# Four weight loads at the start of an attention and gated feed-forward kernel, each issued as two transfers: rows 0 to 119 and rows 120 to 127

## The chip, the core and the metric

The kernel runs on one core of a Trainium2 chip. A core has a matrix engine (PE, with its weight loads shown apart as PEld), a vector engine (DVE), a scalar engine (ACT), a general engine (POOL, called gpsimd in the code) and a queue engine (SP), each with its own stream of instructions. They meet through semaphores. Transfers between the chip's main memory and the core's on-chip memory run on 16 DMA engines. The on-chip memory has 128 rows, called partitions; a tile's first dimension is the row.

The metric is the device time of one execution in microseconds. For the kernel before it is the median of three runs.

## The reference

For each of 8 batches b and 8 heads, with 576 positions, head size 64 and 32 memory slots:

```
a    = softmax(phi, over the 576 positions)            # 576 x 32
k_m  = a^T k ;  v_m = a^T v                            # 32 x 64 each
attn = softmax(q k_m^T / 8, over the 32 slots)         # 576 x 32
x    = attn v_m                                        # 576 x 64
```

The heads of a position are put side by side to a row of 512, which gives 4608 rows. On these a gated feed-forward block is computed, with an inner width of 1536:

```
out = (silu(x @ w_gate) * (x @ w_val)) @ w_out
```

All inputs and the output are float32.

## The kernel before

x is never formed. Since x = attn v_m for each head, the kernel multiplies v_m into the gate and value weights first: U = v_m W is small (32 slots of 8 heads against 1536 columns), and attn U is then the gate or the value. The function `u_round` (L460) makes U: its products (L472) write the tiles p_u from t_kT, the transposed memories, and W, the weights. `gv_half` (L509) makes gate and value, p_g and p_v, from t_A (attn) and t_U (L515), ACT applies silu (L532), DVE multiplies (L538). `products` (L689) multiplies the result by w_out by a scheme with fewer products than the plain one (L727), whose sums of operands POOL makes (L560, L603).

The order of the work is written out by hand, engine by engine in program order; nothing moves an instruction later on. The body first loads what batches 0 and 1 need (L885 to L916), with filler products on PE (`warm`, L867) where PE would otherwise stand idle, then runs batches 0 and 1 together (L921 to L971), and then batches 2 to 7 in a loop (L996).

The gate and value weights lie in main memory as 512 x 1536. They are loaded in three chunks of 512 columns, as bfloat16, by `load_w` (L128), from POOL's queue, since the type changes on the way. In on-chip memory a chunk has 128 rows and, in each row, four runs (the index i: row 128 i + p of the weights goes to partition p). Chunk 0 alone is split in two halves of 256 columns, so that the first products can start sooner:

```python
    for half in range(2):
        for which in range(2):
            load_w(which, 0, half)
    for c in range(1, NCH):
        for which in range(2):
            load_w(which, c)
```

The order on POOL's queue is therefore: k of batch 0, q of batch 0, k of 1, q of 1, v of 0, v of 1 (L99, L108, L103), then the first gate half, first value half, second gate half and second value half of chunk 0, then chunks 1 and 2 of gate and value, and then loads of w_out (L153), k, phi and v for batch 2. The framework gives POOL's transfers eight semaphores in turn. A transfer waits, on POOL, until the one eight places before it has landed; POOL goes through its stream in order, so all that is behind it waits too.

The first readers of W are the products of `u_half` (L836): L954 reads the first gate half, L956 reads the first value half and then both for batch 1, L963 reads the second halves for both batches, and `u_item(0, 1)` in L968 reads chunk 1, gate before value.

Of the kernel before, what the change touches and what calls it, by code (L numbers as in the profile page):

```python
# [14 lines left out]
def kernel(  # L15
# [19 lines left out]
    nc = tc.nc  # L35
# [13 lines left out]
    CH = 512  # L49
# [74 lines left out]
    W = {}  # L124
# [3 lines left out]
    def load_w(which, c, half=None):  # L128

        src = (moe_w_gate, moe_w_val)[which]  # L130
        split = half is not None
        if not half:
            W[which, c] = wpool.tile(
                [128, 2, NP, HC] if split else [128, NP, CH], BF16,
                tag=f"W{which}{c}", name=f"W{which}{c}",
            )
        f0, n = (half * HC, HC) if split else (0, CH)
        nc.gpsimd.dma_start(  # L138
            out=W[which, c][:, half] if split else W[which, c],
            in_=src[:, c * CH + f0:c * CH + f0 + n].rearrange("(i p) f -> p i f", p=128),  # L140
        )

    def w_part(which, c, i, g, halves):

# [760 lines left out]
# [6 lines that stand above are left out]
# [207 lines left out]
```

## Time and profile before

| What | Value |
|---|---|
| Median of three runs | 233.52 us (233.19 to 233.64) |
| The profiled execution, first to last instruction | 231.4 us |
| What lies around that span, by the median | 2.1 us |
| PE busy | 221.6 us, 96% of the span |
| DVE, ACT, POOL busy | 185.1, 171.7, 140.8 us |
| Granted clock of the matrix engine | 0.997 |
| A half chunk of gate or value weights | 256 KB on chip, 512 KB in main memory |
| Issue on POOL to landing, half chunks (median) | gate 19.3 us, value 18.7 us |
| One issue of a weight load on POOL | 0.74 to 0.77 us |

Times in the profile count from the first instruction. A line of the timeline has the start, the length, the engine, the source line, the operation, what it writes and reads, and, in brackets, how long the engine stood idle before it and what ended the idle time. The chain that ended last is followed back from the last instruction: at each step to what released it. The digits of the DMA row are the mean busy share of the 16 engines in tenths, in 40 slices of 5.8 us. POOL's busy time includes its issues of transfers.

### The profile page before, as it was taken

The numbers are of one execution on the slowest core, as the hardware profiler recorded it, in microseconds if no ns is written. First come the engines' busy times: TensorE is split into PE (matmuls) and PEld (weight loads), VectorE is DVE, ScalarE is ACT, GpSimd is POOL, SyncE is SP. The second block draws the span as 40 slices with busy tenths as digits, with TensorE's granted clock in tenths as the row PEclk, the third lists the DMA queues.
The fourth block names the chain that finished last, engine by engine and source line by source line (L and its number), as shares of the span: only waits on it lengthen the run. The fifth ranks groups of instructions, "written<-read, shape, count | busy, mean of one in ns | idle before, by whom it ended". The sixth has DMA issues, their size and how long they took to land.

```text
span 231.4 us, 7210 instructions
## 1 busy us (share of the span) xinstructions
PE 221.6 (96%) x2825; PEld 169.8 (73%) x2825; DVE 185.1 (80%) x423; ACT 171.7 (74%) x365; POOL 140.8 (61%) x190
## 2 busy tenths in 40 slices
PE   6987799999999999999999999999999999999993
PEld 2544476778887777878788787887788778878882
DVE  4245789999966799989997668998999899977732
ACT  2777898988447989968896658978898789677310
POOL 8422427998199049765977689464845394039291
PEclk9999999999999999999999999999999999999998
DMA  6999999999996992999299946994014502202125
GB/s 214 210 211 206 199 207 207 221 245 268 205 225 175 256 256 49 223 204 184 71 223 191 226 134 115 252 236 89 28 65 114 104 0 95 91 10 84 31 85 160
DMA packets 36674, 36.84 MB, mean 159 GB/s; under 512 B 14624, under 2 KB 31008, under 8 KB 36640
## 3 DMA queue, kind: packets, MB, share of 16 engines
q0 software_dynamic: 16272, 22.42, 52.5%
q1 hardware_dynamic: 19600, 13.18, 22.9%
q10 hardware_dynamic: 768, 0.79, 1.1%
q8 instruction: 22, 0.36, 0.6%
q14 instruction: 12, 0.10, 0.1%
HBM read 42.47 MB, written 9.44 MB: 224 GB/s over the span
## 4 chain that ended last, share of the span: by engine, by line
PE 86%; DMA 9%; POOL 2%; ACT 1%; issue 0%; DVE 0%; POOLq 0%
PE p_g L515 21%; PE p_os L727 21%; PE p_v L515 20%; PE p_oc L727 10%; DMA W<-in_moe_w_val_dram 9%; PE p_oa L727 5%; PE p_u L472 5%; PE p_kv L230 2%; PE p_g L396 1%; POOL t_kv L99 1%; POOL t_kv L103 1%; PE p_q L383 0%; POOL t_q L108 0%; ACT t_qT L337 0%; POOL W L138 0%
## 5 line engine op out<-in xcount | busy, mean ns | idle before, releaser
L538 DVE TENSOR_TENSOR t_h<-t_sg,p_v 128x288 bf16<-128x288 bf16 x192 | 81.8, 451 | 14.1 <-PE p_v L515 7.0
L515 PEld LDWEIGHTS <-t_U 128*128 128x128 bf16 x768 | 73.9, 98 | 21.2 <-issue 3.5
L532 ACT ACTIVATE t_sg<-p_g 128x288 bf16<-128x288 f32 x192 | 73.3, 424 | 17.1 <-PE p_g L515 11.4
L515 PE MATMUL p_g<-t_A,t_U 128*128 128x288 bf16 x384 | 77.0, 286 | 0.0
L515 PE MATMUL p_v<-t_A,t_U 128*128 128x288 bf16 x384 | 77.0, 286 | 0.0
L727 PEld LDWEIGHTS <-t_S 128*128 128x128 bf16 x384 | 37.5, 98 | 4.5 <-issue 0.2
L603 POOL TENSOR_TENSOR t_S<-t_h 128x512 bf16<-128x512 bf16 x17 | 19.7, 1157 | 32.7 <-DVE t_h L538 31.2
L727 PEld LDWEIGHTS <-t_h 128*128 128x128 bf16 x288 | 27.1, 98 | 8.6 <-issue 5.0
L492 ACT CAST t_U<-p_u 128x512 bf16<-128x512 f32 x51 | 27.0, 605 | 6.6 <-PE p_u L472 6.6
L727 PE MATMUL p_os<-t_T,t_S 128*128 128x256 bf16 x192 | 23.7, 273 | 0.0
L560 POOL TENSOR_TENSOR t_S<-t_S,t_h 128x512 bf16<-128x512 bf16 x17 | 19.6, 1156 | 1.3
L560 POOL TENSOR_TENSOR t_S<-t_h 128x512 bf16<-128x512 bf16 x16 | 18.4, 1152 | 0.0
L560 POOL TENSOR_TENSOR t_S<-t_h,t_S 128x512 bf16<-128x512 bf16 x16 | 18.4, 1152 | 0.0
L472 PE MATMUL p_u<-W,t_kT 64*32 64x512 bf16 (+1 forms) x416 | 15.3, 363 | 1.2 <-DMA W<-in_moe_w_gate_dram 0.6
L496 DVE CAST t_U<-p_u 128x512 bf16<-128x512 f32 x21 | 13.6, 683 | 1.9 <-PE p_u L472 1.9
L727 PE MATMUL p_os<-t_T,t_h 128*128 128x256 bf16 x96 | 14.8, 273 | 0.0
L875 PE MATMUL p_warm<-bones 128*128 128x512 bf16 x44 | 12.5, 421 | 1.7 <-DVE bones L897 1.7
L452 DVE TENSOR_TENSOR t_A<-t_E,t_lz 128x576 bf16<-128x576 bf16 x16 | 11.4, 740 | 0.7 <-ACT t_lz L428 0.7
L727 PE MATMUL p_oc<-t_T,t_S 128*128 128x256 bf16 x96 | 11.9, 273 | 0.0
L727 PE MATMUL p_oa<-WO,t_h 128*128 128x256 bf16 x96 | 11.8, 273 | 0.0
L727 PE MATMUL p_oc<-WO,t_S 128*128 128x256 bf16 x96 | 11.8, 272 | 0.1
L727 PE MATMUL p_os<-WO,t_h 128*128 128x256 bf16 x96 | 11.8, 273 | 0.0
(107 smaller groups left out, 308.3 us busy)
## 6 DMA issues: line engine op xcount, KB each, us to landing
out_dram<-t_o SPq DMA_DIRECT2D x11, 512.0 KB, 3.0
t_kv<-in_k_dram POOLq DMA_DIRECT2D x8, 576.0 KB, 10.5
t_q<-in_q_dram POOLq DMA_DIRECT2D x8, 576.0 KB, 8.4
t_kv<-in_v_dram POOLq DMA_DIRECT2D x8, 576.0 KB, 14.7
t_phi<-in_phi_dram POOLq DMA_DIRECT2D x6, 576.0 KB, 8.1
out_dram<-t_o SPq DMA_DIRECT2D x10, 256.0 KB, 4.5
WO<-in_moe_w_out_dram POOLq DMA_DIRECT2D x3, 512.0 KB, 19.2
W<-in_moe_w_gate_dram POOLq DMA_DIRECT2D x2, 512.0 KB, 16.5
```

Source lines behind the costliest of these rows:

```text
L230: nc.tensor.matmul(p[g][32 * i:32 * i + 32, 0:n], lhsT=phi_of(b, g, j, i), rhs=kvs[b][64 * g:64 * g + 64, w0:w1, i, j * D:(j + 1) * D], st ...
L452: nc.vector.tensor_tensor(out=a, in0=es.pop((b, g)), in1=lzs.pop((b, g)), op=ALU.mult)
L472: nc.tensor.matmul(p[g][32 * i:32 * i + 32, o:o + n], lhsT=kTs[b][64 * g:64 * g + 64, 2, 32 * i:32 * i + 32], rhs=w_part(w, c, i, g, halve ...
L492: nc.scalar.copy(out=t, in_=p)
L496: nc.vector.tensor_copy(out=t, in_=p)
L515: nc.tensor.matmul(p[:, 0:HALF], lhsT=Us[b, c, g][:, o // 2, which, 128 * (o % 2):128 * (o % 2 + 1)], rhs=atts[b, g][:, r], start=(g == 0) ...
L532: nc.scalar.activation(out=sg, in_=gate[:, 0:HALF], func=AF.Silu)
L538: nc.vector.tensor_tensor(out=dst, in0=sg, in1=val[:, 0:HALF], op=ALU.mult)
L560: eng.tensor_tensor(out=out, in0=x, in1=y, op=ALU.subtract)
L603: eng.tensor_tensor(out=t[:, 0], in0=A21, in1=A22, op=ALU.add)
L727: nc.tensor.matmul(mine[home][:, u], lhsT=lhs(c, m, u), rhs=rhs(c, m), start=fresh and u == 0, stop=(k == 5), skip_group_check=u == 1 or n ...
L875: nc.tensor.matmul(p[:, 0:128 * a], lhsT=bones, rhs=x.to_broadcast([128, a, 128]) if a > 1 else bones, start=True, stop=True,)
```

## The change

Where `load_w` loads a half chunk, it issues two transfers in place of one, the first for partitions 0 to 119 and the second for partitions 120 to 127. Source, destination, type and total bytes are the same. Whole chunks are loaded by one transfer as before. In all, four transfers become eight.

```diff
         f0, n = (half * HC, HC) if split else (0, CH)
-        nc.gpsimd.dma_start(
-            out=W[which, c][:, half] if split else W[which, c],
-            in_=src[:, c * CH + f0:c * CH + f0 + n].rearrange("(i p) f -> p i f", p=128),
-        )
+        dst = W[which, c][:, half] if split else W[which, c]
+        rows = src[:, c * CH + f0:c * CH + f0 + n].rearrange("(i p) f -> p i f", p=128)
+        for part in (slice(0, 120), slice(120, 128)) if split else (slice(0, 128),):
+            nc.gpsimd.dma_start(out=dst[part], in_=rows[part])
```

In program order POOL then has four more transfers between v of batch 1 and chunk 1. With eight semaphores in turn, the transfers behind wait for other ones than before: the 120 rows of the first value half wait for k of batch 0 (the whole first value half had waited for none), and chunk 1 of the gate weights waits for the 120 rows of the first gate half (it had waited for k of batch 1). The other whole chunks and the next loads likewise wait for a part of a half chunk; from the third load of w_out on, each transfer waits for the same earlier one as before. Products that read rows 64 to 127 wait for the second transfer also. The order and number of all other instructions is unchanged on every engine.

## The prediction

> **What bounds the kernel now.** I read the page's busy shares first, then the chain that ended last in order of time, then PE's timeline around the place where that chain leaves PE, and last the timeline of POOL, which issues these loads. The chain says where a microsecond is still worth a microsecond.
>
> ```profile
> PE 221.6 (96%) x2825; PEld 169.8 (73%) x2825; DVE 185.1 (80%) x423; ACT 171.7 (74%) x365; POOL 140.8 (61%) x190
> DMA  6999999999996992999299946994014502202125
> ```
>
> ```profile
> 6.04 0.72 POOL W L138
> 6.75 19.95 DMA W<-in_moe_w_val_dram
> 26.71 0.04 issue
> 26.75 0.52 PE p_u L472 x24
> 27.27 1.09 PE p_g L515 x8
> ```
>
> PE is the bound from 26.75 us on: the windows 26.75 to 54, 54 to 100 and 100 to 228 us have PE busy for 27.25 of 27.25, 45.90 of 46.00 and 127.60 of 128.00 us. Before that the chain is a single DMA, the first half chunk of the value weights, issued at 6.75 and waited for until 26.75. Whatever moves that landing moves the end by as much, as nothing behind it has room to take it up. The DMA row shows that the queues are full over the same time.
>
> ```profile
> 24.67 0.61 PE L875 MATMUL p_warm<-bones 128*128 128x512 bf16 x2
> 25.92 0.30 PE L472 MATMUL p_u<-W,t_kT 64*32 64x256 bf16 x8 [0.65 <-DMA W<-in_moe_w_gate_dram]
> 26.75 0.52 PE L472 MATMUL p_u<-W,t_kT 64*32 64x256 bf16 x24 [0.52 <-DMA W<-in_moe_w_val_dram]
> ...
> 29.75 0.63 PE L472 MATMUL p_u<-W,t_kT 64*32 64x256 bf16 x32
> ...
> 34.70 0.62 PE L472 MATMUL p_u<-W,t_kT 64*32 64x512 bf16 x16
> ```
>
> PE has nothing left at 25.28 (24.67 + 0.61), waits 0.65 us for the first gate half and 0.52 us for the first value half: 1.17 us is all that any earlier landing could give. The next two groups that read weights, at 29.75 and 34.70, start without a wait.
>
> ```profile
> 6.02 0.76 POOL L138 DMA_DIRECT2D W<-in_moe_w_gate_dram  x1
> 6.75 0.77 POOL L138 DMA_DIRECT2D W<-in_moe_w_val_dram  x1
> 9.19 0.75 POOL L138 DMA_DIRECT2D W<-in_moe_w_gate_dram  x1 [1.67 <-DMA t_kv<-in_k_dram]
> 12.00 0.74 POOL L138 DMA_DIRECT2D W<-in_moe_w_val_dram  x1 [2.06 <-DMA t_q<-in_q_dram]
> 14.82 0.74 POOL L138 DMA_DIRECT2D W<-in_moe_w_gate_dram  x1 [2.08 <-DMA t_kv<-in_k_dram]
> 18.40 0.74 POOL L138 DMA_DIRECT2D W<-in_moe_w_val_dram  x1 [2.83 <-DMA t_q<-in_q_dram]
> ```
>
> POOL keeps eight of its transfers in flight: the ninth, at 9.19, waits until the first has landed, and so on. Between issue and landing of the weights lie 15.5 to 20.0 us (the view of the tile W): they stand in a full queue.
>
> The trace also records sixteen completions for each transfer, one a DMA engine. Those of four weight transfers (us):
>
> ```
> first gate half   24.0 to 24.3 (fourteen), 25.1, 25.8
> first value half  25.3 to 25.6 (fourteen), 26.5, 26.7
> second value half 27.9 to 28.4 (fourteen), 29.2, 29.4
> second value chunk 33.1 to 33.4 (thirteen), 34.2, 34.5, 34.5
> ```
>
> PE waits for the last of sixteen. Fourteen engines are 1.1 us ahead of the sixteenth. The reason is in the records of the queue of instruction fetches: one 16 KB packet of 0.95 us at 14.63 and another of 0.94 us at 23.70. Up to the transfer that lands at 14.5 us no engine is behind; after the first packet one is by 0.8, after the second two are, and a third after the packet at 31.48. So the late engines are whichever served a fetch.
>
> **The change, part by part.** *Packets.* Each half chunk is 128 rows by four runs, 512 packets of 512 B (the four make the 2048 such packets of the queue), 32 an engine. Packets of an engine start 41 ns apart, and 32 of them are the 1.3 us by which the landings above follow each other. The same 512 packets are sent after the change. What moves is who sends them. No transfer of 120 or of 8 rows is in this trace. Its nearest row is the 128-row transfer, whose rows go evenly, eight to an engine; by it 120 rows fill fifteen engines as before and the sixteenth has none, and the 8 rows are one more row (four packets, 0.164 us) on each of eight engines. That is the value I take. The lower end is a gain: the engine without rows is a late one. The upper end is eight rows on one engine, or 120 rows on eight: 1.31 us a half chunk.
>
> *Completions.* A transfer ends with a 4 B packet on each engine, 21 ns in the queue. One more a half chunk: 0.02 us.
>
> Together a late engine among those eight has its landing later by 0.185 us a half chunk: 0.37 us at the first value half, 0.74 us at the second and at everything behind it.
>
> *PE.* The first value half ends at 26.73 + 0.37 = 27.10 and PE starts 0.37 later. The second value half is read from 29.87 and lands at 29.43: 0.44 us of room, and PE itself is 0.37 later, so 0.74 fits in 0.81. The second value chunk is read from about 34.99 (34.70 and the eight gate products before it, 0.28) and lands at 34.54: 0.45 of room, plus 0.37, holds 0.74 too. The four added semaphore waits on PE are met by then at no cost; if they were not, each is the landing already counted. The third chunk is read at 43.38 and lands at 39.6: covered by nearly 4 us.
>
> *POOL and its queue.* Four more issues, each between 0.55 us (the q load of 128 packets) and 0.77 us (512 packets). Their place in the eight in flight matters more. The first value half must now wait for the first k (issued at 9.19, before 6.75), the second gate half goes at 14.82 and 18.40, the second value half at 21.29 and 24.11, and the first whole gate chunk no longer at 14.82 but when the 120 rows of the first gate half have landed, 26.07. Behind it on POOL stand nine more loads, at 0.75 us each issued by 33 to 35, and no computing until 36.99. The queue must not run dry: the fourteen early engines end the second value half at 28.4. The first packet of a load into an empty queue came 1.3 us after its issue began (72.27 to 73.56), so the chunk issued at 26.07 starts at about 27.5, with 0.9 us in hand. Of an engine that did run dry, only a late one would count, and those have 1.1 us more work. I cost it at nothing; the cover is this 0.9 + 1.1 us. From the third load of w_out on (issued at 32.21), each load waits for the same earlier one as before. SP's first transpose waits for a q load that lands at 61.3 and for PE, and its output is read after 90 us: 0.74 later costs nothing.
>
> *Sum.* 0 for issue, 0.33 for packets, 0.04 for completions: 0.37 us on the span of 231.4, 231.8. The median of the timed runs stands 2.1 us above that span (233.52 against 231.4), which the change does not touch: 233.9 us, +0.16%.
>
> [...]
>
> **The rivals.** *It is hidden.* The late engines may be among the eight without an added row. Then the landing moves by the completions alone, 0.04 us, and the worst left is a third late engine at the second value chunk, 0.74 less the room of 0.45: 0.04 to 0.3 us, 233.6 to 233.8. For it: the trace does not name engines. Against: two late engines must both be spared.
>
> *It is faster.* The engine that loses its rows is a late one. One alone gives little: with the sixteenth completion of the first value half gone the fifteenth still stands at 26.5, a gain of 0.2 us at most. Only if both late engines are spared, for instance because the idle place moves from transfer to transfer, is the landing that of the other fourteen, 25.6 + 0.37 = 26.0: 0.75 us less, 232.8. It decides when the last completion comes before 26.25. For it: 1.1 us of lag really is there. Against: it is two engines, which change with the fetches.
>
> *The spread is uneven.* If 120 rows ran on eight engines (fifteen rows each), or the eight rows on one, the worst engine has 1.31 us more for each half chunk, 5.2 at the second value chunk; less 0.45 of room 4.8 us, or 3.7 where that engine was none of the late ones: 237.2 to 238.3. For it: a row count that is no power of two; against: 128 rows are spread evenly.
>
> *The queue runs dry.* If the small issues are much slower than 0.77 us, or the first half lands late, the first whole chunk is late by x. Up to about 2.4 us that is covered as worked out above, beyond it PE waits by the rest at 34.99: some 0.5 to 1.2 us, 234.0 to 234.7.
>
> **How the numbers follow.** About 0.2% (0.47 us) is what a measurement of this kernel can tell from no change; the three runs of before span 0.45 us. My forecast, a late engine with an added row, has 0.42: 233.5 to 234.4 on its own, so that 0.25 of it lies within 0.2% and 0.17 above. Hidden 0.18, all within. Faster 0.16, of which 0.14 beyond the bound. Uneven 0.16 and dry 0.08, all slower. So faster 0.14, same 0.45, slower 0.41. The range runs from the full relief (232.8, and 0.1 of spread) to 235.0, above the dry queue; the uneven case is left out.
>
> **What will show it.** Right: PE's first p_u group of values starts at 27.0 to 27.2, the group at 29.75 is later by the same amount and still has no wait, the POOL row for the first whole gate chunk stands near 26, and PE has as much work after it as before. Two late completions of sixteen, some 0.2 us later for each half chunk. Wrong: a start before 26.5 (relief), a wait on W before the groups that stood at 29.75 and 34.70 (uneven), a stretch between 27 and 30 us in which the DMA row falls (dry). What I know least is which engines get the eight rows; the fetches may also fall on other moments in other executions, which would move the lag of 1.1 us itself.

## The result, and the profile after

The changed kernel takes 234.06 us (median of 11 runs, 233.51 to 235.2) against 233.23 us for the kernel before on the same chip (11 runs, 233.06 to 233.64): 0.83 us longer, a ratio of 1.0035 with a 95% interval of 1.0025 to 1.0045. The sign and the mechanism of the forecast held, the size did not: 0.37 us were forecast. That the time still fell near the forecast of 233.9 is in part luck: that was counted from a median of three runs, 233.52, which stands 0.3 us above the 11.

The profiled execution took 233.92 us, with a span of 232.1 us, 0.7 us more than the span before. From its page, the busy shares, the DMA row and the packets:

```profile
PE 222.2 (96%) x2825; PEld 169.9 (73%) x2825; DVE 185.2 (80%) x423; ACT 171.5 (74%) x365; POOL 143.1 (62%) x194
DMA  6999999999997993899199965994023602202125
DMA packets 36994, 36.84 MB, mean 159 GB/s; under 512 B 14944, under 2 KB 31328, under 8 KB 36960
```

The work is the same but for POOL's four more issues. The page of the kernel before has 36674 packets: 320 more now, all of them under 512 B, and as many bytes. The chain that ended last, from its beginning (start, length, what):

```profile
1.25 7.78 DMA t_kv<-in_k_dram
9.03 0.28 issue
9.31 17.81 DMA W<-in_moe_w_val_dram
27.12 0.04 issue
27.16 0.78 PE p_u L472 x24
27.94 1.09 PE p_g L515 x8
```

As before it leaves the DMA at the first value half. That it now begins with k, for which the issue at 9.31 waited, looks like a new cause; an experiment below (112 and 16 rows) has the same issues and no loss clear of the noise. What counts is where the chain turns to PE. PE's timeline there:

```profile
25.10 0.60 PE L875 MATMUL p_warm<-bones 128*128 128x512 bf16 x2
26.05 0.50 PE L472 MATMUL p_u<-W,t_kT 64*32 64x256 bf16 x8 [0.35 <-DVE t_kT L339]
27.16 0.78 PE L472 MATMUL p_u<-W,t_kT 64*32 64x256 bf16 x24 [0.61 <-DMA W<-in_moe_w_val_dram]
...
30.43 0.63 PE L472 MATMUL p_u<-W,t_kT 64*32 64x256 bf16 x32
...
35.37 0.63 PE L472 MATMUL p_u<-W,t_kT 64*32 64x512 bf16 x16
```

The weight loads of the group of 24, before and after:

```profile
26.75 0.24 PEld L472 LDWEIGHTS <-t_kT 64*32 64x32 bf16 x23 [0.71 <-issue]
27.42 0.24 PEld L472 LDWEIGHTS <-t_kT 64*32 64x32 bf16 x23 [1.06 <-DMA W<-in_moe_w_val_dram]
```

The group of 24 starts 0.41 us later than before (26.75), close to the forecast of 27.10. But it also takes 0.78 us where it took 0.52. One product, on rows 0 to 63, starts at 27.16, when the 120 rows have landed; the second, on rows 64 to 127, starts at 27.42, when the 8 rows are there. The merged PE line hides this second wait in a longer group; the line of the weight loads shows it. The next two groups are 0.68 and 0.67 us later than before, without a wait. So the first value half is late by 0.67 us, and nothing after it is worse. POOL's timeline of the loads:

```profile
9.31 0.78 POOL L141 DMA_DIRECT2D W<-in_moe_w_val_dram  x1 [1.91 <-DMA t_kv<-in_k_dram]
12.12 0.55 POOL L141 DMA_DIRECT2D W<-in_moe_w_val_dram  x1 [2.03 <-DMA t_q<-in_q_dram]
...
26.20 0.79 POOL L141 DMA_DIRECT2D W<-in_moe_w_gate_dram  x1 [1.01 <-DMA W<-in_moe_w_gate_dram]
26.98 0.76 POOL L141 DMA_DIRECT2D W<-in_moe_w_val_dram  x1
```

The first whole gate chunk is issued at 26.20 (forecast 26.07). An issue of 8 rows took 0.55 us, one of 120 took 0.78. The completions of the sixteen engines, from the trace (us):

```
                             before                       after
first value half (120 rows)  25.3 to 25.6, 26.5, 26.7     24.8, 24.8, 25.3 to 25.8, 27.0, 27.1
  its 8 rows                                              25.0, 25.0, 25.6 to 26.0, 27.2, 27.4
second value half, 8 rows    27.9 to 28.4, 29.2, 29.4     27.6, 27.8, 27.9, 28.5 to 28.9, 29.9
gate chunk 1                 30.5 to 30.9, 31.7, 31.9     31.3 to 31.6, 32.2, 32.3, 32.6
```

(The second value half of before is one transfer of 128 rows.) Of the first gate half one engine is ahead (23.3, the next at 24.0), of the first value half two (24.8, the next at 25.3), of the 8 rows of the second value half three (27.6 to 27.9, the next at 28.5). The trace does not name engines; this is read as the engine without rows not always being the same. At the first value half two engines are late, as before, and later still. The fourteenth completion is 0.40 us later than before (26.02 for 25.62), and the last is 1.36 us behind the fourteenth where it was 1.09: 0.40 and 0.27 make the 0.67. At the second value half only one engine is left late. In the stretch from 27 to 29 us the queue thins out; the windows by engine (busy us, the granted clock, the DMA share and GB/s at the end), of the kernel before:

```profile
27.00:29.00 2.00, 2.00 (x39) 1.46 (x16) 1.78 (x4) 1.85 (x6) 1.37 (x2) 1.00 1.34 203
```

and of the changed one:

```profile
27.00:29.00 2.00, 1.84 (x34) 1.15 (x34) 1.90 (x4) 1.30 (x4) 2.00 (x3) 1.00 1.24 147
```

147 GB/s instead of 203: the first whole chunk came too late to keep the queue full. Its first packets start at 27.7, when an engine reaches them, but some of them take up to 0.98 us, where before each takes 0.10. This is not a matter of the engines without rows alone: with 112 and 16 rows, where no engine runs ahead, it is 146 GB/s. Everything behind in the queue then lands some 0.7 to 1.1 us later (v of batch 2 at 55.2 instead of 54.3).

### The profile page after: what moved, and what is told of

Read it like the earlier page. It is cut to its first block, busy times and chain, and to the rows that moved or that the text cites. A ratio compares the mean times of both kernels' runs of the same rounds, so it can differ in the third digit from the quotient of the medians.

```text
span 232.1 us, 7214 instructions
## 1 busy us (share of the span) xinstructions
PE 222.2 (96%) x2825; PEld 169.9 (73%) x2825; DVE 185.2 (80%) x423; ACT 171.5 (74%) x365; POOL 143.1 (62%) x194
## 4 chain that ended last, share of the span: by engine, by line
PE 86%; DMA 11%; ACT 1%; issue 0%; DVE 0%; POOLq 0%
PE p_g L515 21%; PE p_os L727 21%; PE p_v L515 20%; PE p_oc L727 10%; DMA W<-in_moe_w_val_dram 8%; PE p_u L472 5%; PE p_oa L727 5%; DMA t_kv<-in_k_dram 3%; PE p_kv L230 2%; PE p_g L396 1%; PE p_q L383 0%; ACT t_qT L337 0%; ACT t_p L752 0%; DVE t_q L339 0%; PE p_S L258 0%
## 5 line engine op out<-in xcount | busy, mean ns | idle before, releaser
L472 PE MATMUL p_u<-W,t_kT 64*32 64x512 bf16 (+1 forms) x416 | 15.8, 363 | 1.0 <-DMA W<-in_moe_w_val_dram 0.6
```

What stands on the lines that cost most here:

```text
L472: nc.tensor.matmul(p[g][32 * i:32 * i + 32, o:o + n], lhsT=kTs[b][64 * g:64 * g + 64, 2, 32 * i:32 * i + 32], rhs=w_part(w, c, i, g, halve ...
```

## The experiments

Two theories stood against each other at first. *Rows:* rows are dealt out whole, and what costs is that 120 and 8 rows do not fill sixteen engines evenly. *Transfers:* the four more transfers, their issues, or the changed window of eight in flight cost. Twelve kernels were run, four of them on each of three chips; the kernel before ran beside each four.

**The changed kernel again (e0_again).** No edit.

> The changed kernel once more, all four half chunks as 120 and 8 rows, for a second profile beside the others of this group. Theory rows (the cost is the extra packets that a late DMA engine sends ahead of the first value half, and PE's wait for the second of the two transfers): PE's first value products again later than in the kernel before by 0.3 to 0.7 us, the 8 rows landing some 0.2 us behind the 120; 233.8 to 234.3 us. Theory window (eight transfers in flight, so that the first whole chunk is issued 11 us later and the DMA queue runs thin): the same total, but with PE waiting for the second value chunk.

Measured: 234.19 us (12 runs, 233.53 to 235.73) against 233.59 for the kernel before (35 runs, 233.02 to 234.43): ratio 1.0026 (1.0007 to 1.0044). The loss, 0.60 us, is there on a second chip, with a wide spread.

**112 and 16 rows (e1_112_16).**

```diff
-        for part in (slice(0, 120), slice(120, 128)) if split else (slice(0, 128),):
+        for part in (slice(0, 112), slice(112, 128)) if split else (slice(0, 128),):
```

> Each half chunk again as two transfers, but of rows 0 to 111 and 112 to 127, both multiples of sixteen. The number of transfers, their issues on POOL and their places among the eight in flight are those of the changed kernel. Theory rows: every engine keeps its eight rows, only completions of 0.02 us a transfer are added, so 0.04 to 0.1 us above the kernel before, 233.3 to 233.4 us, and no burst of short packets on an idle engine. Theory window, and a fixed cost for each added transfer: as slow as the changed kernel, 0.7 to 0.9 us above before.

Measured: 233.69 us, ratio 1.0001 (0.9989 to 1.0013). The line of its page:

```profile
DMA packets 36739, 36.84 MB, mean 159 GB/s; under 512 B 14689, under 2 KB 31073, under 8 KB 36705
```

That is 65 packets more than before; the completions of four more transfers make 64. The 256 further short packets of the changed kernel are gone. Both row counts divide evenly over sixteen engines. As many transfers, in the same order of issues, cost 0.10 us by the medians, which is not clear of nothing (-0.26 to +0.30 us), where the changed kernel beside it lost 0.60 (0.16 to 1.03). The two intervals overlap; the run with 124 and 4 rows below bears the theory of rows out at a size far beyond the noise. As the cause of the bulk of the loss, the theory of transfers falls.

One part of it stays. The first whole gate chunk is issued late here too (26.05), and the queue thins out without any engine running ahead:

```profile
27.00:29.00 2.00, 1.98 (x36) 1.33 (x35) 1.63 (x3) 1.42 (x4) 2.00 (x3) 1.00 1.16 146
```

In the two runs that follow, which split only half of the loads and issue that chunk at 21.4 and 21.7, the same stretch moves 202 and 199 GB/s, as before the change. So the thin queue comes with the late issue, and not with the uneven rows.

**Only the first, only the second halves split (e2_first, e3_second).**

```diff
-        for part in (slice(0, 120), slice(120, 128)) if split else (slice(0, 128),):
+        for part in (slice(0, 120), slice(120, 128)) if half == 0 else (slice(0, 128),):
```

The other one has `half == 1`.

> Only the first halves (the first gate half and the first value half) as 120 and 8 rows, the second halves whole. Theory rows: nearly the whole cost, 0.5 to 0.8 us, because these are the transfers ahead of the wait that sets the end. Theory window: none, since the first whole chunk now waits for v of batch 0 and is issued near 21 us. A fixed cost per transfer: half, 0.4 us.

> Only the second halves as 120 and 8 rows. Theory rows: the first value half lands as before, the second up to 0.4 us later into 0.44 us of room, so 0 to 0.1 us. Theory window: none, the first whole chunk is issued near 21 us. A fixed cost per transfer: 0.4 us if the room behind the first value half did not cover it.

Measured: first halves 233.81 us, ratio 1.0011 (0.9998 to 1.0023); second halves 233.65 us, 1.0003 (0.999 to 1.0016). The medians stand 0.22 and 0.06 us above before, 0.28 together, and the whole change 0.60 beside them. The order is the expected one (what PE waits for costs, what is covered does not), but neither differs surely from no change; the first halves were expected to cost 0.5 to 0.8 us and came out lower. The sum is less than the whole, though by the spread of these runs that could be chance. One thing that needs both is the late issue of the first whole chunk.

Where that can cost shows at 59 us, where PE transposes q of batch 2 (p_q, L383). In the kernel before, q lands at 58.63 and PE comes at 59.12, without a wait:

```profile
59.12 0.84 PE L383 MATMUL p_q<-ident,t_q 128*128 128x128 bf16 x12
```

In the profile of the changed kernel run again:

```profile
59.58 0.84 PE L383 MATMUL p_q<-ident,t_q 128*128 128x128 bf16 x12 [0.23 <-DMA t_q<-in_q_dram]
```

Here q lands at 59.53. The queue carries its delay of 0.9 us from the start for 30 us; PE in this execution was late by 0.17 only, and the room of 0.49 us is used up. The profile of 112 and 16 rows, with the same late chunk and no uneven rows, has such a wait too; q lands at 59.93 there:

```profile
59.98 0.84 PE L383 MATMUL p_q<-ident,t_q 128*128 128x128 bf16 x12 [0.35 <-DMA t_q<-in_q_dram]
```

**Fixing the place of the idle engine (f0_start0, f1_start4, f2_start8, f3_start12).** The theory, an assumption: the engine that gets no rows is the next in a turn that goes on from one execution to the next, so that the spread of the changed kernel comes from where the turn stands. A small transfer of 4, 8 or 12 rows, which nothing reads, is put ahead of the loads and another behind the last, so that by this theory all executions start alike:

```diff
+    def turn(n):
+        t = consts.tile([16, 16], FP32, tag=f"turn{n}", name=f"t_turn{n}")
+        nc.gpsimd.dma_start(out=t[0:n], in_=phi[0, 0, 0:n, 0:16])
```

The four have, ahead and behind: none and 4, 4 and none, 8 and 12, 12 and 8 rows.

> The changed kernel, and behind its last load one more transfer of 4 rows of 64 B that nothing reads. Theory turning: in the completions of the changed kernel one engine runs ahead after the first half chunk, two after the second, three after the fourth, so that the engines without rows change from transfer to transfer, 15 on for 120 rows and 8 on for 8 rows, 92 on in an execution, and the next execution begins elsewhere. With the 4 rows it is 96, a multiple of 16, and each execution begins in the same place as its first. Then the spread (2.2 us in twelve runs of the changed kernel on this chip) falls to that of the kernel before (1.4 us in 35) and the median lies near the first, profiled executions, 233.5 to 233.9 us. If the places do not turn between executions, spread and median stay as in the changed kernel, 234.0 to 234.3 with runs above 235. [...]

> The changed kernel with a transfer of 4 rows of 64 B, read by nothing, ahead of all loads of POOL: 96 places in an execution, so that every execution begins four places on. The eight in flight are as in the changed kernel, as this transfer lands long before its place is used again. Theory turning: a spread like that of the kernel before and a median of its own, between 233.4 and 235.5, and in the profile other engines are ahead and other ones late. Theory of no turning: 234.0 to 234.3 as in the changed kernel, with runs above 235.

> The changed kernel with 8 rows of 64 B ahead of all loads and 12 rows behind the last: 112 places in an execution, so that every execution begins eight places on. Theory turning: a spread like that of the kernel before and a median of its own, between 233.4 and 235.5. Where it is slow, the profile shows where: PE waits for the first value half by more than in the kernel before, or for the second value half, or for the second value chunk. Theory of no turning: 234.0 to 234.3 as in the changed kernel.

> The changed kernel with 12 rows of 64 B ahead of all loads and 8 rows behind the last: 112 places, every execution begins twelve places on. Theory turning: a median of its own between 233.4 and 235.5 with a small spread, and the mean of the four starting places is that of the changed kernel, 234.2. Theory of no turning: as the changed kernel.

Measured, against 233.5 us (35 runs, standard deviation 0.30): 234.3 (deviation 0.28), 234.65 (0.48), 233.98 (0.36), 234.22 (0.80); ratios 1.0033, 1.0049, 1.0025 and 1.0043, each within about 0.002. All four lose. Only one has the small spread that the theory asks for, and the last falls into two groups, seven runs from 233.76 to 234.33 and then four in a row from 235.49 to 235.68. The theory is not shown. Three of the four long runs list a granted clock of 0.989 to 0.992 where the first seven list 0.997 to 1.000, but the fourth lists 0.998; what sets the two groups stays open. The profiles are of use in another way: the last one has the largest wait for q of all,

```profile
60.16 0.84 PE L383 MATMUL p_q<-ident,t_q 128*128 128x128 bf16 x12 [0.74 <-DMA t_q<-in_q_dram]
```

where PE had been only 0.23 us late until then.

**Taking the second place away (g1_after_qfirst, and on the kernel before, g2_before_qfirst).** q of batch 2 is loaded ahead of phi of batch 3:

```diff
-        (0, 0): lambda: (load_phi(3, nc.gpsimd), load_q(2)),
+        (0, 0): lambda: (load_q(2), load_phi(3, nc.gpsimd)),
```

> The changed kernel with one line swapped: q of batch 2 is loaded ahead of phi of batch 3 instead of behind it, so that it should land about 2 us earlier than the 59.7 us of the changed kernel. Theory of two places (the late landing of the first value half, and again q of batch 2, which PE's transposes at p_q read about 59 us in): the second place is gone, no wait stands before the p_q transposes, VectorE's drift against the kernel before is as large at the end as it is at 28 us, and the median is 0.2 to 0.5 us above the kernel before, with few runs above 234.4. Rival, the first place alone carries the loss: the median stays 0.6 to 0.8 us above the kernel before, with the same tail up to 235.

> The kernel before with the same swapped line, nothing split: the control for the run beside it. Two places: q of batch 2 had 0.5 us of room here (landed 58.6, read 59.12), so the median stays within 0.2 us of the kernel before; a loss of its few runs near 234.4 would say that the same place makes those. Rival, the swap itself is worth something (the queue or PE's order changes by it): the median moves by more than 0.3 us, and the difference of the run beside it has to be read against this one.

Measured, against 233.31 us (23 runs, 232.97 to 234.43): changed kernel with the swap 233.83 (12 runs, 233.49 to 234.89), ratio 1.002 (1.0007 to 1.0034); kernel before with the swap 233.43, 1.0001 (0.9987 to 1.0014). The swap by itself does nothing, and the changed kernel still loses 0.52 us to before, 0.40 to its control. That is just above what was expected of two places (0.2 to 0.5) and just below what was expected of one alone (0.6 to 0.8). Against the 0.60 and 0.83 us of the changed kernel without the swap, the second place would be worth between 0.1 and 0.4 us of the median, but the intervals overlap, and these runs cannot tell it from nothing. The expected end of the tail did not come: the profiled execution is itself the longest, 234.89 us, and its lines say where that lies:

```profile
27.64 0.73 PE L472 MATMUL p_u<-W,t_kT 64*32 64x256 bf16 x24 [1.33 <-DMA W<-in_moe_w_val_dram]
...
60.22 0.84 PE L383 MATMUL p_q<-ident,t_q 128*128 128x128 bf16 x12
```

No wait at p_q (q landed at 57.66), and all of the loss at the first value half: its last rows landed at 27.81. Two engines were behind the others by 1.6 and 1.8 us there, where they were 0.8 and 1.1 behind in the kernel before; the first of them was behind fourteen of the others by 1.6 us already when v of batch 1 landed (0.8 before), after an instruction fetch at 14.83. The kernel before has such a fetch at 14.63; why the lag behind one is 1.6 us and behind the other 0.8 the trace does not show, nor that the fetch makes it.

Beside each other, twelve profiles show how strictly the first place works. The second column is the last of the sixteen completions of the first value half (of its second transfer, where there are two), the third how much later VectorE's first multiply of gate and value starts than in the kernel before, the fourth the same past 77 us, behind the second place:

| Kernel | Landed, us | Later at 28 us | Later past 77 us |
|---|---|---|---|
| before | 26.71 | 0 | 0 |
| before, q first | 26.57 | -0.14 | -0.14 |
| second halves only | 26.86 | 0.16 | 0.15 |
| first halves only | 26.86 | 0.16 | 0.16 |
| 112 and 16 rows | 27.14 | 0.44 | 0.86 |
| changed | 27.38 | 0.67 | 0.67 |
| changed, again | 26.87 | 0.16 | 0.46 |
| changed, none and 4 rows | 27.34 | 0.63 | 0.72 |
| changed, 4 and none | 27.24 | 0.53 | 0.57 |
| changed, 8 and 12 | 27.38 | 0.67 | 0.79 |
| changed, 12 and 8 | 26.93 | 0.23 | 1.03 |
| changed, q first | 27.81 | 1.10 | 1.10 |

The third column is the second less 26.71, within 0.02 us, in every row: PE's start follows the last landing one to one. The three kernels with an undivided first value half land at 26.71 on average, the seven changed ones at 27.28, 0.57 us later; past the second place those seven are 0.76 us late on average, against medians that stood 0.48 to 1.15 us above before. One profile says little: the seven, whose first halves are loaded alike, land anywhere from 26.87 to 27.81. The row of 112 and 16 is the exception among the even ones: 0.44 us late at the first place with no uneven rows. It is of an execution of 234.07 us, the second longest of its twelve, so the profiles alone do not tell it from the seven; the medians do that.

**124 and 4 rows (g3_124_4).**

```diff
-        for part in (slice(0, 120), slice(120, 128)) if split else (slice(0, 128),):
+        for part in (slice(0, 124), slice(124, 128)) if split else (slice(0, 128),):
```

> Rows 0 to 123 and 124 to 127 in place of 0 to 119 and 120 to 127, all four half chunks. Theory that whole rows are dealt out to a number of engines that divides the row count: 124 rows go as 31 rows on each of four engines, 124 packets of 41 ns (5.1 us) where there were 32 (1.3 us); the first value half lands some 6 to 8 us later, and with the four half chunks the median is 3 to 7 us above the kernel before; twelve engines without rows show as short packets, far more than the 320 of the changed kernel. Rival, rows are spread as evenly as the count allows (124 on sixteen engines, seven or eight each): it costs no more than the changed kernel, 0.4 to 0.9 us, with packets added by completions alone.

Measured: 241.4 us (4 runs, 240.31 to 242.21), ratio 1.0334 (1.0301 to 1.0367): 8.1 us longer. From its page:

```profile
DMA packets 42882, 36.86 MB, mean 153 GB/s; under 512 B 20832, under 2 KB 37216, under 8 KB 42848
```

6208 more packets than before. The trace does not name engines, but a count explains the number: if the 124 rows lie on four engines, 31 each, an engine sends 124 packets; if each of the other twelve sends as many short ones, and likewise 4 for the 4 rows, with 16 completions that is 1488 + 48 + 16 = 1552 a half chunk, and four times that is 6208. The same count for 120 rows (one engine idle, 32) and 8 rows (eight idle, 4 each) gives 32 + 32 + 16 = 80, and four times that is the 320 seen. The completions agree: of the first gate half twelve engines are done by 25.2, four at 28.2 to 28.5. PE's timeline:

```profile
28.63 1.63 PE L472 MATMUL p_u<-W,t_kT 64*32 64x256 bf16 x32 [2.90 <-DMA W<-in_moe_w_gate_dram]
30.19 2.10 PE L515 MATMUL p_g<-t_A,t_U 128*128 128x288 bf16 x8
...
36.15 1.22 PE L472 MATMUL p_u<-W,t_kT 64*32 64x256 bf16 x32 [1.38 <-DMA W<-in_moe_w_gate_dram]
...
43.24 0.62 PE L472 MATMUL p_u<-W,t_kT 64*32 64x512 bf16 x16
```

and its windows (the last three figures: granted clock, DMA share, GB/s):

```profile
25.80:27.30 1.50, 0.00 (x0) 0.00 (x0) 0.38 (x2) 0.76 (x1) 0.00 (x0) 1.00 1.35 108
27.40:34.20 6.80, 5.57 (x49) 3.13 (x50) 3.11 (x6) 3.49 (x8) 3.03 (x4) 0.50 1.17 125
34.30:37.60 3.30, 1.92 (x39) 0.90 (x38) 1.30 (x3) 0.77 (x2) 1.21 (x2) 1.00 1.43 166
37.70:41.00 3.30, 3.30 (x16) 2.12 (x14) 1.81 (x5) 2.40 (x6) 2.41 (x4) 0.50 1.23 205
41.10:43.00 1.90, 1.90 (x17) 1.52 (x16) 1.46 (x5) 1.60 (x4) 0.74 (x1) 1.00 1.23 204
```

The expectation had the count of engines right and the path wrong. The first value half landed at 29.4, 2.7 us later, not 6 to 8, and only 0.9 us behind the first gate half (28.5), where 124 packets of 41 ns behind those of the gate on the same engines would be 5.1. That is read as gate and value on different groups of four engines, side by side. PE's two waits, 4.28 us, are 3.1 more than the 1.17 of before. Most of the rest is clock. The granted clock fell to 0.50 at 27.4, inside the wait of 2.90 us, and stayed there to 34.2; it was 1.00 to 37.6, 0.50 again to 41.0, and 1.00 from then on. The eight gate products behind the first weight group took 2.10 us where they took 1.15. The same products between the first weight group and the one at 43.24 took 13.2 us without the wait between them, where they had taken 8.3. Of these 5.0 us about 4.5 are half of the 9.0 us in which PE was busy at half the clock, an estimate from the stretches above. The 5.0 us, the 3.1 us and 0.45 that PE was late already at 25.12 make the 8.5 us by which everything past 43 us is later in this execution.

**A version that might beat both (g4_v1_later).** The kernel before with the swap of q, and v of batch 1 loaded behind the first halves, its work on PE moved behind them:

```diff
     load_v(0)
-    load_v(1)
-    for half in range(2):
-        for which in range(2):
-            load_w(which, 0, half)
+    for which in range(2):
+        load_w(which, 0, 0)
+    load_v(1)
+    for which in range(2):
+        load_w(which, 0, 1)
...
-    v_direct(1, "vvvv")
-    warm(8)
...
-    run([u_half(0, (0,), 0, 0, "va")])
+    run([u_half(0, (0,), 0, 0, "vv")])
...
-    run([u_half(0, (1,), 0, 0, "va"), u_half(1, (0, 1), 0, 0, "av")])
-    for s in range(4):
+    run([u_half(0, (1,), 0, 0, "vv")])
+    for s in range(3):
         gv_gate(0, s)
+    v_direct(1, "vvvv")
+    gv_gate(0, 3)
...
+    run([u_half(1, (0, 1), 0, 0, "av")])
```

> The kernel before with the swapped line and the loads in another order: v of batch 0, the first gate and value halves, then v of batch 1, then the second halves; PE does the first gate and value halves of batch 0 and its gates, then the work on v of batch 1 that it had done ahead of them. If what bounds the start is the landing of the first value half, that lands by about the 0.7 us earlier that the v load took in the queue ahead of it (64 packets an engine), PE's work of the first value half starts at 25.9 to 26.2 instead of 26.75, and the time is 0.4 to 0.9 us below the kernel before. If the start is bound by PE, VectorE or the second halves as well, a new wait stands before the work on v of batch 1 or before the second halves, and the time is within 0.3 us or longer.

Measured: 234.73 us (5 runs), ratio 1.0051 (1.0033 to 1.0068), 1.4 us longer than before. PE's timeline:

```profile
23.93 0.41 PE L472 MATMUL p_u<-W,t_kT 64*32 64x256 bf16 x16
24.83 1.18 PE L515 MATMUL p_g<-t_A,t_U 128*128 128x288 bf16 x6 [0.49 <-DVE t_U L498]
26.65 0.76 PE L325 MATMUL p_mT<-t_mphi,t_kv 128*64 128x64 bf16 x36 [0.65 <-DMA t_kv<-in_v_dram]
...
29.68 0.62 PE L515 MATMUL p_g<-t_A,t_U 128*128 128x288 bf16 x2 [0.79 <-ACT t_U L494]
```

The first value half landed at 23.6, 3.1 us earlier (0.7 had been expected), and PE's work on it began 2.8 us earlier; three new waits (the copies of U on DVE and ACT, and v of batch 1, 1.93 us in all) and the moved work itself took more than that back: the group of both second halves starts at 30.96 where it started at 29.75. The rival that was named came true. Nothing run here beats the kernel before.

## Why the prediction was right and wrong

- *The chain leaves the DMA at the first value half, and its landing moves the end one to one:* right, and the table shows it twelve times.
- *Packets, 0.33 us, and completions, 0.04 us, at the first value half; PE 0.37 later:* the mechanism right, the term mis-sized. The packet counts (the 320) fit the spread assumed, 120 rows on fifteen engines and 8 rows one each on eight. The last 8 rows land 0.16 to 0.26 us behind the last of the 120, where four packets of 41 ns and a completion make 0.185. But the whole was 0.67 us in the profile of the changed kernel and 0.57 on average. The step that failed is that the lag of the late engines was taken as the 1.1 us of one profile, the same before and after. For the engines that are not late the term fits: the fourteenth completion is 0.40 us later in the changed kernel's profile, and 0.33 on average over the seven against the three with an undivided half. The lag of the last behind the fourteenth is what came on top: 0.27 us in that profile, 0.24 on average (1.10 for 0.87). It differs from execution to execution (one engine was 0.8 us behind after its first fetch in the profile of before, 1.6 in that of 234.89 us). With landings from 26.87 to 27.81, seven profiles cannot tell 0.57 from 0.37 with much confidence, nor whether the longer lag belongs to the change.
- *PE's start at 27.10:* met (27.16), but by luck: 27.10 was to be the landing of both parts, and 27.16 follows the landing of the 120 rows alone. PE does one product and waits again, until 27.42.
- *0.74 us is covered at the second value half and at the second chunk:* right; no wait at 30.43 and 35.37. The delays were 0.50 us at the half (29.91 for 29.41) and 0.99 at the second value chunk (35.46 for 34.47).
- *POOL costed at nothing, the first whole chunk near 26, the queue with 0.9 us in hand:* the issue came at 26.20, as forecast, but the 0.9 us did not keep the queue full. The sign named for a queue that runs dry, less traffic between 27 and 30 us, came: 147 GB/s for 203, and 146 with 112 and 16 rows. With those rows even the engine that is first has 3.14 us between the second value half and the first whole chunk, where it had 2.58. PE did not wait at the second value chunk for it; it can pay at q of batch 2, and the median of 112 and 16 rows puts it at 0.10 us, not clear of nothing.
- *"0.74 later costs nothing" for the loads further back:* this step was incomplete. It followed q of batch 3 to its first reader, and not q of batch 2, which has 0.49 us of room at 59.12. By the forecast's own numbers, 0.74 late against 0.49 of room and PE 0.37 late, there is no wait; but where PE is late by less than the queue (0.17 against 0.9, 0.23 against 1.5), the difference comes due there: 0.23 and 0.74 us. On average over the seven profiles the loss grows from 0.57 to 0.76 us past this place.
- *The base:* 2.1 us around the span came from setting the median of three runs against the span of one. The profiled executions since stood 1.8 us above their own spans.
- *The rivals:* hidden and faster did not come, though one, two and then three engines ahead can be read as the idle place moving from transfer to transfer, as the second assumed. Of the dry queue the thin stretch came and the wait at the second value chunk did not. Uneven spread: not at 120 and 8, but at 124 and 4 it came, 8.1 us; the argument for it, a count that is no power of two, was the wrong test, since 112 is none either and cost 0.10 us, not clear of nothing.

## What to carry to other kernels

Before a load is cut in two, measure what the row counts do: here 112 and 16 rows cost nothing that could be measured (ratio 1.0001), 120 and 8 some 0.6 to 0.8 us, 124 and 4 8.1 us, with the same bytes and the same number of transfers; only the first pair divides evenly over sixteen engines. When a full queue gets later, follow the delay to every later load that has less room than the delay, tens of microseconds on (here q of batch 2, 0.9 late with 0.49 of room at 59 us), and not only to the next few. And where the last of sixteen landings sets the end, one profile is one draw: the changed kernel landed 0.5 us apart in two executions (27.38 and 26.87), and its variants with the same first loads up to 0.9.

## What the runs showed of the hardware that was not expected

- The split into 120 and 8 rows brought short packets beside its completions: between 20 and 30 us the POOL loads of the changed kernel show 401 packets of 4 B, those of the kernel before 81, and 252 of the 401 took 9 ns, a length that none of the 81 has (of the completions before most took 22 ns). That the engines without rows send them, each as many as the others send packets with data, is read from the counts above, 320 and 6208, which come out exactly so; the trace does not name engines.
- PE started the group of 24 on the part of the tile that had landed and waited inside the group for the rest. The merged PE line shows only a longer group (0.78 us for 0.52); the weight loads show the wait (1.06 us, to 27.42).
- One engine was late after an instruction fetch, a 16 KB packet of 0.95 us at 14.63 in the kernel before, and stayed late while the queue was full: there one is 0.8 us behind at 18 us and still at 24 us, and by way of the last landing this lag is in the end of the kernel. Which engine served which fetch the trace does not name; that the two belong together is read from the moments. They fit: where the fetch came at 14.6 to 16.4 us, q of batch 1 is the first load with a late engine; where it came at 17.4 and 17.6 (112 and 16 rows, 124 and 4 rows), q still landed together and v of batch 0 is the first.
- In one execution the granted clock fell to 0.50 inside a wait of PE of 2.90 us, 1.7 us after PE had stopped, and again 1.5 us after a wait of 1.38 us, for 6.8 and 3.4 us. A wait of 1.33 us in another execution left it at 1.00. What separates the last two these runs do not show.
